# One copy of 64x288 for the partial sums of an output product, four new durations for a planner, and a new instruction order

## The chip, the cores and the metric

The kernel runs on one core of a Trainium2 chip. The metric is device time in microseconds for one launch; several runs are taken and the median is given. The profile is one further execution, recorded by the hardware profiler; its times are in microseconds from the start of its span. TensorE is called PE in the profile (PEld are its weight loads), VectorE DVE, ScalarE ACT, GpSimd POOL, and SP is the engine that issues most of the DMAs.

## The reference, cut to what matters

Two independent computations on the same input `x` (2048 rows of 576 features) are mixed by a gate:

```python
x = A_x
g = sigmoid((x * gate_w).sum(-1, keepdims=True))
a = A(x)      # recurrent, 64 segments
b = B(x)      # ordinary softmax attention
return g * a + (1 - g) * b
```

A is a recurrence. The 2048 rows are cut into 64 segments of 32 rows. Before each segment stand 8 rows of memory, so that 40 rows go in:

```python
for s in range(64):
    h = concat([mem, x[:, 32*s:32*s+32, :]], axis=1)      # 40 x 576
    q, k, v = h @ Wq, h @ Wk, h @ Wv                      # 32 heads of 128
    p = softmax(where(mask, q @ k.T * scale, -1e9))       # 40 x 40 for each head
    o = (p @ v over the heads) @ Wo                       # 40 x 576
    mem = o[:, :8, :]                                     # goes into the next segment
    outs.append(o[:, 8:, :])
```

Only `mem` is passed on: segment s cannot begin with its first 8 rows before the output product of segment s-1 has ended. B is attention over all 2048 rows with 32 heads of 18, and nothing in it depends on A.

## The kernel before, in words

**Two kinds of work in one stream.** A segment of A leaves engines waiting for each other, so the kernel lays B's attention between A's steps. B is 32 chunks (8 groups of 4 heads, times 4 chunks of 512 queries), each of 16 *visits* to 128 keys, 512 visits in all. A visit is `sb` on PE (four matmuls, one for each head, each in its own 32 rows of the array, L932; three write the tile `sb`, one the tile `sp`), then two exponentials on ACT (`ex` 128x1536, L941, and `ey` 128x512, L945), then `ob` on PE (four matmuls in the array's four columns of 32, L955).

**A segment's chain.** Names end in the segment's number, and 0 or 1 in them is the half of the heads.
- `Q0 K0 Q1 K1 V0 V1`, five steps each of four 32-column matmuls of 512 (L1321), into a PSUM bank `pvv`.
- The copy `tm<-pvv` (L540 on DVE, L538 on ACT: both are one helper, `copier`). For Q and K follow a transposing DMA `tt<-tm` (L1411, issued on SP) and a DVE copy `qk<-tt` (L1420); for V one DMA and one copy into `v_sb` (L1360).
- `ph`: scores `psh` (L1435 mask, L1443 products), then an exponential on ACT (L1453). `sm`, `rc`: sums and their reciprocal. `bc`: the reciprocals spread by PE into `prb` (L1487), `nm`: a DVE product (L1498).
- `po`: `pso`, probabilities times values (L1509), `co`: two copies `ot<-pso` of 128x320 (L540 or L538).
- `op`: the output product (L1194). For the first half (`op0`) it is done with two column tiles of 288: four quarters of 32 partitions, of which the two lower hold the sums of the even steps and the two upper those of the odd steps. They have to be added, which is what `halved` does. For the second half (`op1`) it is done with four column tiles of 144, and nothing has to be added.
- `halved` for `op0`: two copies (`su0`, `su1`) bring the upper 64 partitions, 144 columns each, from PSUM to the tile `sum`, and two additions (`tu0`, `tu1`, L1227) add the lower 64 partitions to them. The second half is added by `oc` (`obf<-acc,sum`, L1542).
- `fo`: `pw`, a small fold of the first 8 rows (L1556, L1560) and the DVE product `ht<-pw,keep` (L1568): the memory for the next segment.

The last 8 of the 40 rows do not feed the recurrence. Their output product (`lo`) runs once in four segments and also goes through `halved` (`sl0`, `sl1`, `tl0`, `tl1`, into `lbf`); their projections (`la`, L1025 and L1029) are laid in where there is room.

**What sets the order.** Every operation is first added to a planner, with its engines, a duration in microseconds, its dependencies, a priority, and the buffers it takes and gives back (`tokens_of`: 4 PSUM banks `pb`, 1 `sb`, 2 `sum`, and so on). `Plan.run` then lays the operations out one by one on a clock of its own: at each step it takes the operation that can start first, with priorities among those that start at about the same time. The instructions are emitted in that order, each engine's as one queue. Two numbers are added to the durations: 0.105 when the array's tiling changes (row tiles, column tiles or the whole array, L117), and 0.205 from the end of a PE operation until another engine may use it (L116). Where the plan leaves PE idle it lays in a filler (`warm`, products of a zero tile, L902, planned at 0.216), which keeps PE busy and whose result changes nothing. `TURNS` (L57) has 65 numbers, one for each segment and one ahead: each seeds factors on the priorities and the planner's thresholds until the next segment begins. So any change of one duration can move instructions everywhere behind it.

Two helpers give the planned durations of copies:

```python
def psum_copy(n, narrow=False):
    return ((n / 2 if narrow else n) + 151) / 960.0
def act_time(n):
    return (n + 205) / 1200.0
```

Of the kernel before, what the change touches and what calls it, by code (L numbers as in the profile page):

```python
# [10 lines left out]
FP32 = mybir.dt.float32  # L11
BF16 = mybir.dt.bfloat16
ACT = mybir.ActivationFunctionType
ALU = mybir.AluOpType
# [40 lines left out]
]  # L55
RANK = dict(RANKS[0])
TURNS = [  # L57
    3874553, 4590935, 9148581, 3541498, 535923, 7788852, 3952484, 7153488, 7395194, 8320517, 4368777, 8584864,
    7828412, 8268306, 4467502, 9711640, 4225875, 3218189, 5891388, 9878869, 3366758, 2473878, 665120, 265532,
    2017390, 6740513, 5628863, 269513, 7513788, 1193947, 4221311, 4642080, 2536147, 3044628, 2615070, 8009909,  # L60
    8409899, 7834349, 4105115, 3984977, 6495726, 2668014, 2119719, 693899, 3876392, 7513682, 1436744, 7393048,
    2936900, 4795848, 3391573, 5680957, 6437275, 7165951, 5197151, 4567334, 1419855, 3366056, 6270251,
    7670628, 2126425, 9002684, 6140375, 3882872, 284549,
]
FACTORS = (0.02, 0.1, 0.25, 0.4, 0.55, 0.7, 0.85, 1.0, 1.2, 1.5, 1.9, 2.4, 3.0, 4.0, 6.0, 10.0)
KNOBS = ("switch", "near", "early", "wait", "gap", "cool")
# [44 lines left out]
class Plan:  # L111
# [59 lines left out]
    def add(  # L171
        self, name, engs, dur, fn, deps=(), prio=5.0, mode=None, take=(), give=(), tail=0.0, dmas=0, kb=0.0,
        use=None, pairs=4, alt=None, waits=0.0,
    ):
        op = Op(name, engs, dur, fn, deps, prio, mode, take, give, tail)
        op.dmas, op.kb = dmas, kb
        op.pairs, op.alt, op.form, op.waits = pairs, alt, mode, waits
        op.kind = self.kinds.setdefault(kind_of(name), len(self.kinds))
        op.use = self.ARRAY.get(mode) if use is None else use
        op.seq = len(self.ops)  # L180
        op.slots = {}
        self.ops.append(op)
        return op
# [184 lines left out]
# [6 lines that stand above are left out]
# [3 lines left out]
def kernel(  # L377
# [16 lines left out]
    P = nc.NUM_PARTITIONS  # L394
# [17 lines left out]
    RW = Dm // NF  # L412
# [18 lines left out]
    plan = Plan()  # L431
    add = plan.add
# [29 lines left out]
    for jj in range(2):  # L462
        nc.vector.memset(bsel[64 * jj:64 * jj + 64, jj:jj + 1], 1.0)
    nc.gpsimd.affine_select(
        out=veil[0:64, M:L], in_=veil[0:64, M:L], pattern=[[1, seg]],
# [6 lines left out]
    for j in range(4):  # L472
        r = slice(32 * j, 32 * j + 32)
# [55 lines left out]
    def given(pool, tag, shape, dt):  # L529
        k = plan.slot(tag)  # L530
        return pool.tile(shape, dt, name=tag, tag=f"{tag}{k}", bufs=1)
# [3 lines left out]
    def copier(out_of, in_of):  # L535
        def fn(e):
            if e == "ACT":
                nc.scalar.copy(out=out_of(), in_=in_of())  # L538
            else:
                nc.vector.tensor_copy(out=out_of(), in_=in_of())  # L540
        return fn
# [373 lines left out]
    for gq in range(GB * NQC):  # L915
# [3 lines left out]
        for kb in range(NKB):  # L919
            c = 4 * g + kb // KC  # L920
            o = (kb % KC) * P
            if qc == 0 and kb % KC == 0:
                load_k(c)
                load_v(c)

            def visit(e, c=c, gq=gq, o=o, kb=kb):
                box["sb", gq, kb] = sb = ps_s.tile([P, 3, QC], FP32, name="sb")
                box["sp", gq, kb] = sp = bank([P, QC], FP32, "sp")
                kc, qt_ = kring[c % NKR], qring[gq % NQR]
                for j in range(4):  # L930
                    r = slice(32 * j, 32 * j + 32)
                    nc.tensor.matmul(  # L932
                        sb[:, j, :] if j < 3 else sp[:, :], lhsT=kc[r, o:o + P], rhs=qt_[r, :], start=True, stop=True,
                        tile_position=(32 * j, 0),
                    )

            vi = add(f"sb{gq}.{kb}", "PE", 0.216, visit, [k_of[c], q_of[gq], last_vi], prio=-0.6 if gq < 2 else 0.0, mode="row", take=("sb", "pb"))

            def expo(e, gq=gq, kb=kb):
                box["etb", gq, kb] = etb = given(bint, "etb", [P, 4, QC], BF16)  # L940
                nc.scalar.activation(out=etb[:, 0:3, :], in_=box["sb", gq, kb][:, :, :], func=ACT.Exp, scale=scale_b)  # L941

            def expo4(e, gq=gq, kb=kb):
                etb = box["etb", gq, kb]
                nc.scalar.activation(out=etb[:, 3, :], in_=box["sp", gq, kb][:, :], func=ACT.Exp, scale=scale_b)  # L945

            ex = add(f"ex{gq}.{kb}", "ACT", act_time(1536), expo, [vi], prio=0.0, take=("etb",), give=(("sb", vi, 0),))
            ey = add(f"ey{gq}.{kb}", "ACT", act_time(512), expo4, [ex], prio=0.01, give=(("pb", vi, 0),))

            def values(e, c=c, gq=gq, kb=kb, o=o):  # L950
                if kb == 0:
                    box["ob"] = ps_o.tile([P, QC], FP32, name="ob")
                ob, vc, etb = box["ob"], vring[c % NVR], box["etb", gq, kb]
                for j in range(4):
                    nc.tensor.matmul(  # L955
                        ob[32 * j:32 * j + 32, :], lhsT=vc[:, o + 32 * j:o + 32 * j + 32], rhs=etb[:, j, :],
                        start=(kb == 0), stop=(kb == NKB - 1), tile_position=(0, 32 * j), skip_group_check=True,
                    )
                if kb == NKB - 1:
                    box["ob", gq] = ob  # L960

            va = add(
                f"ob{gq}.{kb}", "PE", 0.216, values, [ex, ey, v_of[c], last_va], prio=-0.5 if gq < 2 else RANK["ob"], mode="col",
                take=("ob",) if kb == 0 else (), give=(("etb", ex, 0),),
            )
            visits[gq, kb] = (vi, ex, va)
            last_vi, last_va = vi, va
            if kb == 0:
                plan.opens.add(va)
            if kb == NKB - 1:  # L970
                plan.closes.add(va)
            if kb == 0:
                first_va = va
            if kb == NKB - 1:
                visits["quse", gq] = vi
            if qc == NQC - 1 and kb % KC == KC - 1:
                visits["kuse", c], visits["vuse", c] = vi, va
# [120 lines left out]
    opened = {}  # L1098
# [73 lines left out]
    plan.tokens_of("tm", 4)  # L1172
    plan.tokens_of("xl", 2)
    plan.tokens_of("obf", 1)
    plan.tokens_of("sum", 2)
    plan.tokens_of("lbf", 1)
    plan.tokens_of("tt", 3)
    plan.tokens_of("xg", 1)
# [30 lines left out]
        return op  # L1209

    def halved(name, state, done, out_of, last_give, prio, held=()):
        lows, sums = [], []

        def low(i):
            def fn(e):
                if i == 0:
                    state["sum"] = given(opened["fix"], "sum", [P, RW], FP32)
                copier(
                    lambda: state["sum"][64 * i:64 * i + 64, :],
                    lambda: state["acc"][64:128, RW * i:RW * i + RW],  # L1220
                )(e)
            return fn

        def both(i):
            def fn(e):
                r = slice(64 * i, 64 * i + 64)
                nc.vector.tensor_tensor(  # L1227
                    out=out_of()[r, :], in0=state["acc"][0:64, RW * i:RW * i + RW], in1=state["sum"][r, :], op=ALU.add,
                )
            return fn  # L1230

        for i in range(2):
            lows.append(add(
                f"s{name[0]}{i}.{name[1:]}", ("DVE", "ACT"), (psum_copy(144), act_time(144)), low(i), [done, *lows], prio=prio,
                take=("sum",) if i == 0 else (),
            ))
        for i in range(2):
            sums.append(add(
                f"t{name[0]}{i}.{name[1:]}", "DVE", 0.308, both(i), [lows[i], *sums], prio=prio, take=held if i == 0 else (),
                give=(("pb", state["op0"], 0), *last_give(lows[0])) if i else (),  # L1240
            ))
        return sums[1], lows[0], sums[0]

    group_end = {}
    pend_lo = []
# [5 lines left out]
    for s in range(n_seg):  # L1251
# [124 lines left out]
        for hf in range(2):  # L1376
# [69 lines left out]
                            start=False, stop=True, tile_position=(0, 32 * i), skip_group_check=True,  # L1446
                        )

            p_ = add(f"ph{hf}.{s}", "PE", 0.365, psh, [*turned, pl], prio=RANK[f"ph{hf}"], mode="col", take=("pb",), use=0.4, pairs=36)
            cur[f"psh{hf}"] = p_  # L1450

            def xp(e, hf=hf, s=s):
# [30 lines left out]
            def bc(e, hf=hf, s=s):  # L1483
                box["prb", s, hf] = pr = bank([P, W8], FP32, "prb")
                for k, o in enumerate(CH):
                    for i in range(4):
# [3 lines left out]
                            rhs=ident[:, :], start=True, stop=True, tile_position=(0, 32 * i), skip_group_check=True,  # L1490
                        )

            b_ = add(f"bc{hf}.{s}", "PE", 0.176, bc, [r_], prio=RANK[f"bc{hf}"],
                     mode="col", take=("pb",), use=0.3, pairs=12)

            def nm(e, hf=hf, s=s):
# [5 lines left out]
            def pso(e, hf=hf, s=s):  # L1502
# [3 lines left out]
                for r in range(8):  # L1506
                    for jj in range(2):
# [4 lines left out]
                            rhs=et[rr, r * L:(r + 1) * L], start=True, stop=True, tile_position=(64 * jj, 0),  # L1512
                        )

            o_ = add(f"po{hf}.{s}", "PE", 0.2, pso, [n_, lv, *pvx], prio=RANK[f"po{hf}"], mode="tall", take=("pb", "pb"), pairs=16, waits=0.15,
                     give=(("tm", evx, 0),))
            cur[f"pso{hf}"] = o_
            for jj in range(2):
# [21 lines left out]

        def ob_cast(e, s=s, st=acc_state, st0=first_half):
            nc.vector.tensor_tensor(  # L1542
                out=opened["obf"][:, s % 4, 0:RW], in0=st["acc"][:, :], in1=st0["sum"][:, :], op=ALU.add
            )

        c1 = add(f"oc{s}", "DVE", 0.308, ob_cast, [mids[1], half_sum], prio=0.3, take=("obf",) if s % 4 == 0 else (),
# [258 lines left out]
```

## Time and profile before

| what | value |
|---|---|
| median of 3 runs | 1424.92 us (1424.34 to 1431.61) |
| profiled execution, its own time | 1423.9 us |
| its span | 1422.0 us, so 1.9 us lie around it |
| PE busy | 1349.8 us, 95% of the span |
| ACT busy | 1097.6 us, 77% |
| DVE busy | 860.2 us, 60% |
| POOL busy | 529.7 us, 37% |
| granted PE clock, mean | 0.996 |
| copies `sum<-acc` 64x144 | 126 on DVE of 310 ns, 34 on ACT of 275 ns |
| additions `sum<-acc,sum` and `lbf<-acc,sum` 64x144 | 160 on DVE of 300 ns |

Busy time of an engine is the union of its instructions. Fillers count as busy, and the ends of matmuls are modelled, so that a PE that is busy 95% is not one that could not do the same work in less. The chain of waits follows the execution back from its last instruction, at each step to what released it.

The span has three stages: projections and preparation up to about 130 us, the 64 segments with B's visits between them from there to about 1395 us, and the final product and the gate's mixing in the last 27 us.

### The profile page before, as it was taken

The page shows a single profiled execution, that of the slowest core. Times are in us where ns is not written, and L with a number is a line of the kernel's source. Part 1 is how long each engine was busy: PE and PEld are TensorE (multiplying, and loading weights), DVE is VectorE, ACT ScalarE, POOL GpSimd, SP SyncE. Part 2 cuts the span into 40 slices and gives each one's busy share as a digit, 9 for nine tenths or more (in the row PEclk, how much of TensorE's full clock was granted, in tenths as well). Part 3 has the DMA queues.
Part 4 walks back from the last instruction along what each step waited for, and adds up shares of the span by engine and source line. Part 5 has one row for each costly group of instructions (what it writes and reads, how often), then busy time and mean ns, then how long its engine had stood idle before and what let it go on. Part 6 is the DMA issues. An engine that isn't in the chain of part 4 may idle for free.

```text
span 1422.0 us, 73418 instructions
## 1 busy us (share of the span) xinstructions
PE 1349.8 (95%) x32607; PEld 717.7 (50%) x32620; DVE 860.2 (60%) x2093; ACT 1097.6 (77%) x1297; POOL 529.7 (37%) x1148
## 2 busy tenths in 40 slices
PE   8999899999999999999999999999999999999998
PEld 4455344555555444555555544555554444444445
DVE  4454466666656656665566666666656666565657
ACT  3478778887887777787877877788777887888884
POOL 8252244234532345332543325333353333432320
PEclk9999999999999999999999999999999999999999
DMA  8887644333424434433433334333335333333335
GB/s 260 249 326 213 134 81 68 63 69 73 78 61 73 57 78 72 71 63 63 83 66 70 64 67 77 73 61 71 63 81 89 59 54 56 66 64 54 54 76 176
DMA packets 343993, 130.66 MB, mean 92 GB/s; under 512 B 296495, under 2 KB 330023, under 8 KB 343675
## 3 DMA queue, kind: packets, MB, share of 16 engines
q1 hardware_dynamic: 315155, 80.47, 29.3%
q0 software_dynamic: 26368, 43.31, 11.2%
q8 instruction: 255, 4.18, 1.3%
q10 hardware_dynamic: 2152, 2.19, 0.5%
q14 instruction: 63, 0.52, 0.1%
HBM read 52.74 MB, written 31.12 MB: 59 GB/s over the span
## 4 chain that ended last, share of the span: by engine, by line
PE 67%; DVE 14%; DMA 11%; issue 3%; ACT 3%; SPq 1%; DVEq 0%; POOL 0%; ACTq 0%; POOLq 0%
PE pvv L1321 25%; PE sb L932 8%; PE acc L1194 8%; DMA tt<-tm 7%; PE ob L955 6%; PE pv L1025 4%; DVE ot L540 3%; PE pso L1509 3%; PE pq L734 2%; DVE tm L540 2%; DMA v_sb<-tm 2%; ACT etb L941 2%; PE pv L1029 2%; DVE sum L540 2%; PE psh L1443 2%
## 5 line engine op out<-in xcount | busy, mean ns | idle before, releaser
L941 ACT ACTIVATE etb<-sb 128x1536 bf16<-128x1536 f32 x512 | 743.6, 1452 | 227.0 <-PE sp L932 156.6
L540 DVE CAST tm<-pvv 128x512 bf16<-128x512 f32 x359 | 247.3, 689 | 238.1 <-PE pvv L1321 233.2
L1321 PEld LDWEIGHTS <-ht 128*32 128x32 bf16 x7680 | 200.8, 96 | 217.2 <-issue 38.5
L945 ACT ACTIVATE etb<-sp 128x512 bf16<-128x512 f32 x512 | 304.1, 594 | 0.6 <-PE sp L932 0.6
L932 PE MATMUL sb<-qch,kch 32*128 32x512 bf16 x1536 | 201.1, 385 | 4.1 <-ACT etb L941 3.4
L955 PE MATMUL ob<-etb,vch 128*32 128x512 bf16 x2048 | 200.5, 384 | 0.5 <-DVE tq L983 0.4
L932 PE MATMUL sp<-qch,kch 32*128 32x512 bf16 x512 | 196.6, 384 | 3.1 <-DMA kch<-ktd 1.7
L1194 PE MATMUL acc<-wo,ot 128*32 128x288 bf16 (+1 forms) x6144 | 169.1, 248 | 6.7 <-DVE ot L540 4.8
L1321 PE MATMUL pvv<-wq_m,ht 128*32 128x512 bf16 x2048 | 145.2, 380 | 2.9 <-DVE ht L1568 0.8
L1321 PE MATMUL pvv<-wv_m,ht 128*32 128x512 bf16 x2048 | 144.0, 380 | 0.3 <-DVE tm L540 0.3
L1321 PE MATMUL pvv<-wk_m,ht 128*32 128x512 bf16 x2048 | 142.8, 380 | 1.4 <-DVE vl L540 0.6
L1194 PEld LDWEIGHTS <-ot 128*32 128x32 bf16 x6144 | 110.8, 96 | 49.5 <-DVE ot L540 26.2
L540 DVE CAST ot<-pso 128x320 bf16<-128x320 f32 x206 | 94.9, 483 | 67.2 <-PE pso L1509 63.4
L932 PEld LDWEIGHTS <-kch 32*128 32x128 bf16 x2048 | 54.5, 91 | 144.6 <-issue 129.2
L1270 POOL COPY ht<-xg 128x96 bf16<-128x96 bf16 x64 | 18.9, 296 | 278.2 <-PE pvv L1321 273.6
L1420 DVE COPY qk<-tt 128x512 bf16<-128x512 bf16 x256 | 77.3, 304 | 40.1 <-DMA tt<-tm 36.6
L851 POOL DMA_DIRECT2D qch<-qtd x120 | 61.9, 523 | 96.2 <-PE sp L932 91.5
L851 POOL DMA_DIRECT2D otd<-stage x124 | 63.2, 517 | 56.2 <-DVE stage L998 39.6
L1498 DVE TENSOR_TENSOR et<-et,prb 128x320 bf16<-128x320 bf16 x128 | 62.0, 485 | 36.5 <-PE prb L1487 29.7
L1453 ACT ACTIVATE et<-psh 128x320 bf16<-128x320 f32 x128 | 56.3, 441 | 32.9 <-PE psh L1443 30.4
L955 PEld LDWEIGHTS <-vch 128*32 128x32 bf16 x2048 | 53.7, 94 | 50.2 <-issue 40.2
L1360 DVE COPY v_sb<-tm 32x512 bf16<-32x512 bf16 x226 | 70.8, 313 | 8.4 <-ACT tm L538 3.2
(161 smaller groups left out, 1972.3 us busy)
## 6 DMA issues: line engine op xcount, KB each, us to landing
v_sb<-tm SPq DMA_DIRECT2D x256, 32.0 KB
xl<-qkd SPq DMA_DIRECT2D x64, 128.0 KB
qkd<-vl POOLq DMA_DIRECT2D x48, 128.0 KB
wo<-in_A_Wo_dram POOLq DMA_DIRECT2D x4, 1152.0 KB
vgd<-vt SPq DMA_DIRECT2D x32, 128.0 KB
wv_m<-in_A_Wv_dram POOLq DMA_DIRECT2D x4, 1024.0 KB
wq_m<-in_A_Wq_dram POOLq DMA_DIRECT2D x4, 1024.0 KB
wk_m<-in_A_Wk_dram POOLq DMA_DIRECT2D x4, 1024.0 KB
```

Source lines behind the costliest of these rows:

```text
L540: nc.vector.tensor_copy(out=out_of(), in_=in_of())
L851: dma(out=rows_, in_=pads) if out else dma(out=pads, in_=rows_)
L932: nc.tensor.matmul(sb[:, j, :] if j < 3 else sp[:, :], lhsT=kc[r, o:o + P], rhs=qt_[r, :], start=True, stop=True, tile_position=(32 * j, 0),)
L941: nc.scalar.activation(out=etb[:, 0:3, :], in_=box["sb", gq, kb][:, :, :], func=ACT.Exp, scale=scale_b)
L945: nc.scalar.activation(out=etb[:, 3, :], in_=box["sp", gq, kb][:, :], func=ACT.Exp, scale=scale_b)
L955: nc.tensor.matmul(ob[32 * j:32 * j + 32, :], lhsT=vc[:, o + 32 * j:o + 32 * j + 32], rhs=etb[:, j, :], start=(kb == 0), stop=(kb == NKB - ...
L1025: nc.tensor.matmul(out_, lhsT=lw, rhs=rw, start=(c == 0), stop=(c == NF), skip_group_check=wide)
L1194: nc.tensor.matmul(acc[32 * q:32 * q + 32, :], lhsT=o[:, slot, t0:t0 + CT], rhs=wo[:, h, d:d + n], start=(first and s_ == (s_ % 2 if wide ...
L1321: nc.tensor.matmul(pv[32 * j:32 * j + 32, :], lhsT=ht[:, cc, :], rhs=rw, start=(c == 0), stop=(c == NF), tile_position=(0, 32 * j), skip_g ...
L1360: move(out=opened["v_sb"][64 * (j // 2):64 * (j // 2) + CT, o:o + 512], in_=tm[32 * j:32 * j + CT, :],)
L1420: eng.tensor_copy(out=opened["qk"][:, hf, a, 0:16 * L].rearrange("p (j i t) -> p j i t", i=4, t=L)[:, :, :, 0:CT], in_=box["tt", s, a, hf] ...
L1498: nc.vector.tensor_tensor(out=et[:, :], in0=et[:, :], in1=box["prb", s, hf][:, :], op=ALU.mult)
```

## The change

Three things are changed. In `halved`, one copy of 64x288 takes the place of the two of 64x144; the tile `sum` is 288 wide instead of 144, there is one of it instead of two, and both additions wait for the one copy. The planner's durations of `sb`, `ph`, `bc` and `po` are set to other values. And `TURNS` has 65 new numbers. The lines that follow in the file have moved up by 9.

```diff
 TURNS = [
-    3874553, 4590935, 9148581, 3541498, 535923, 7788852, 3952484, 7153488, 7395194, 8320517, 4368777, 8584864,
...
+    7952103, 9687964, 5516313, 4619848, 2331426, 9781478, 6767540, 9438387, 4494518, 2665133, 7827388,
...
-            vi = add(f"sb{gq}.{kb}", "PE", 0.216, visit, [k_of[c], q_of[gq], last_vi], prio=-0.6 if gq < 2 else 0.0, mode="row", take=("sb", "pb"))
+            vi = add(f"sb{gq}.{kb}", "PE", 0.3, visit, [k_of[c], q_of[gq], last_vi], prio=-0.6 if gq < 2 else 0.0, mode="row", take=("sb", "pb"))
...
-    plan.tokens_of("sum", 2)
+    plan.tokens_of("sum", 1)
...
     def halved(name, state, done, out_of, last_give, prio, held=()):
-        lows, sums = [], []
-
-        def low(i):
-            def fn(e):
-                if i == 0:
-                    state["sum"] = given(opened["fix"], "sum", [P, RW], FP32)
-                copier(
-                    lambda: state["sum"][64 * i:64 * i + 64, :],
-                    lambda: state["acc"][64:128, RW * i:RW * i + RW],
-                )(e)
-            return fn
+        def low(e):
+            state["sum"] = given(opened["fix"], "sum", [P, 2 * RW], FP32)
+            copier(lambda: state["sum"][0:64, :], lambda: state["acc"][64:128, :])(e)
 
         def both(i):
             def fn(e):
-                r = slice(64 * i, 64 * i + 64)
+                cols = slice(RW * i, RW * i + RW)
                 nc.vector.tensor_tensor(
-                    out=out_of()[r, :], in0=state["acc"][0:64, RW * i:RW * i + RW], in1=state["sum"][r, :], op=ALU.add,
+                    out=out_of()[64 * i:64 * i + 64, 0:RW], in0=state["acc"][0:64, cols], in1=state["sum"][0:64, cols], op=ALU.add,
                 )
             return fn
 
-        for i in range(2):
-            lows.append(add(
-                f"s{name[0]}{i}.{name[1:]}", ("DVE", "ACT"), (psum_copy(144), act_time(144)), low(i), [done, *lows], prio=prio,
-                take=("sum",) if i == 0 else (),
-            ))
+        first = add(
+            f"s{name[0]}0.{name[1:]}", ("DVE", "ACT"), (psum_copy(288) + 0.05, act_time(288)), low, [done], prio=prio, take=("sum",),
+        )
+        sums = []
         for i in range(2):
             sums.append(add(
-                f"t{name[0]}{i}.{name[1:]}", "DVE", 0.308, both(i), [lows[i], *sums], prio=prio, take=held if i == 0 else (),
-                give=(("pb", state["op0"], 0), *last_give(lows[0])) if i else (),
+                f"t{name[0]}{i}.{name[1:]}", "DVE", 0.34, both(i), [first, *sums], prio=prio, take=held if i == 0 else (),
+                give=(("pb", state["op0"], 0), *last_give(first)) if i else (),
             ))
-        return sums[1], lows[0], sums[0]
+        return sums[1], first, sums[0]
...
-            p_ = add(f"ph{hf}.{s}", "PE", 0.365, psh, [*turned, pl], prio=RANK[f"ph{hf}"], mode="col", take=("pb",), use=0.4, pairs=36)
+            p_ = add(f"ph{hf}.{s}", "PE", 0.41, psh, [*turned, pl], prio=RANK[f"ph{hf}"], mode="col", take=("pb",), use=0.4, pairs=36)
...
-            b_ = add(f"bc{hf}.{s}", "PE", 0.176, bc, [r_], prio=RANK[f"bc{hf}"],
+            b_ = add(f"bc{hf}.{s}", "PE", 0.24, bc, [r_], prio=RANK[f"bc{hf}"],
...
-            o_ = add(f"po{hf}.{s}", "PE", 0.2, pso, [n_, lv, *pvx], prio=RANK[f"po{hf}"], mode="tall", take=("pb", "pb"), pairs=16, waits=0.15,
+            o_ = add(f"po{hf}.{s}", "PE", 0.14, pso, [n_, lv, *pvx], prio=RANK[f"po{hf}"], mode="tall", take=("pb", "pb"), pairs=16, waits=0.15,
...
-                out=opened["obf"][:, s % 4, 0:RW], in0=st["acc"][:, :], in1=st0["sum"][:, :], op=ALU.add
+                out=opened["obf"][:, s % 4, 0:RW], in0=st["acc"][:, :], in1=st0["sum"][:, 0:RW], op=ALU.add
```

The copy reads the upper 64 partitions over all 288 columns and writes the tile's lower 64 partitions; the second addition reads columns 144 to 287 of both operands and writes partitions 64 to 127, columns 0 to 143.

## The prediction

> **What bounds the kernel now.** I read the page's busy shares first, then the chain of waits, then the segment stage piece by piece. One per cent of this kernel is 14 us; about 0.5% (7 us) is what a measurement of it can tell from no change.
>
> ```profile
> PE 1349.8 (95%) x32607; PEld 717.7 (50%) x32620; DVE 860.2 (60%) x2093; ACT 1097.6 (77%) x1297; POOL 529.7 (37%) x1148
> PE 67%; DVE 14%; DMA 11%; issue 3%; ACT 3%; SPq 1%; DVEq 0%; POOL 0%; ACTq 0%; POOLq 0%
> PE pvv L1321 25%; PE sb L932 8%; PE acc L1194 8%; DMA tt<-tm 7%; PE ob L955 6%; PE pv L1025 4%; DVE ot L540 3%; PE pso L1509 3%; PE pq L734 2%; DVE tm L540 2%; DMA v_sb<-tm 2%; ACT etb L941 2%; PE pv L1029 2%; DVE sum L540 2%; PE psh L1443 2%
> ```
>
> PE looks full, but the chain is on PE for 67% only: DVE, DMA and ACT hold the other third. The recurrence is a loop in which PE's queue, in its fixed order, meets waits. How much, the chain in order of time shows (start, length, what):
>
> ```profile
> 607.10 1.29 PE pvv L1321 x24
> 608.39 0.32 PE sb L932 x3
> 608.72 0.00 PE sp L932
> 608.72 0.33 PE pvv L1321 x4
> 609.05 0.21 PE ob L955 x4
> 609.26 1.29 PE pvv L1321 x24
> ```
>
> Six groups of four column products take 1.29 us, so one occupies PE 0.215 us; a visit's scores 0.32, which is 0.215 and a change of tiling of 0.105; the group behind them pays 0.105 again. In the same way I read, for operations that wait for nothing, 0.36 for `ph`, 0.177 for `bc`, 0.196 and a change for `po`, 0.25 for a step of `op`, 0.28 for a `la` unit of five. I laid these over the order of PE operations between `fo0` and `fo62` (170.1 to 1372.2 us): 1089 us of work, fillers included, in 1202 us. So 113 us, 1.8 us for each segment of 19.4, PE waits with nothing even to fill. That, and not PE's work, is what an order can change.
>
> The changed copies are in the tail that closes the loop. In DVE's timeline:
>
> ```profile
> 698.15 0.89 DVE L540 CAST ot<-pso 128x320 bf16<-128x320 f32 x2 [0.76 <-PE pso L1509]
> 699.07 0.65 DVE L540 COPY sum<-acc 64x144 f32<-64x144 f32 x2
> 699.75 0.63 DVE L1227 TENSOR_TENSOR sum<-acc,sum 64x144 f32<-64x144 f32 x2
> 700.49 0.31 DVE L1542 TENSOR_TENSOR obf<-acc,sum 128x144 bf16<-128x144 f32 x1
> ```
>
> PE's timeline has the products of the second half over by 699.96; `obf` starts at 700.49 because DVE is at the partial sums until 700.38. `fo` and the next segment's projections wait for `obf`. The reader sees here that DVE, at 60%, is the bound for a stretch of each segment.
>
> **The change part by part.**
>
> *One copy for two.* A copy of 64x144 takes 310 ns on DVE. A PSUM copy of 128x288 (`vt<-pvb`) takes 458 ns, and partitions do not count, so 64x288 takes 0.46. [...] In some segments the copy isn't the last thing before `obf`, and `op1` comes in as the next wait; I take −7. The two additions stay at 0.30 each; the new 0.34 and the 0.05 on the copy exist in the plan only.
>
> On ACT there were 34 such copies of 275 ns; built from its source, the changed program has 11. ACT rows of 275 (144) and 430 (320) put 288 at 0.40, so 9.4 us become 4.4. ACT mostly waits for scores and not the reverse, so this lies beside: −1 (0 to −5). DVE gets 69 copies where it had 126: 39.1 to 31.7 us.
>
> *One `sum` tile for two.* The copy for `lo` may not start while `op0`'s sums are held from the copy to `obf`, 1.4 us or more, and `lo` holds one of four PSUM banks meanwhile; what else waits in DVE's queue then is its next work. This happens in 16 groups at most, so 0 to 16 x 1.4 = 22 us. The plan knows of the tile and lays `lo` elsewhere, so I take a low +1.
>
> *Four durations.* "Set to the trace" is half true. Scores at 606.16 let the exponential start at 606.65, 0.49 later. The plan had 0.216 and its 0.205 for handing over, 0.42; now it has 0.505. `psh` at 612.34 lets its exponential start at 612.97, 0.63 against 0.57 before and 0.615 now. So the hand-over to other engines is now right. But a duration is also how long PE is held, and there the old numbers were right (0.216, 0.365, 0.176, 0.2 against my 0.22, 0.36, 0.177, 0.196) and three new ones are long: 512 x 0.084 + 128 x 0.045 + 128 x 0.064 − 128 x 0.06 = 49 us that PE won't need, 0.8 for each segment. The real PE reaches its next operation earlier than planned, and then waits.
>
> *The order.* From the programs: fillers (four products of the zero tile each) 174 to 138, changes of tiling 1330 to 1292, 37 `la` parts from one full form to four column forms (20 weight loads where there were 5, +0.003 each by the rows, nothing). Between `fo0` and `fo62` the same rows give 1081.8 us of PE work where there were 1089.3: −7.5. On POOL there are 14 more `v_sb` copies at 0.62, on DVE 14 fewer at 0.31; SP's DMA into the same tile takes 3 to 5 us beside them, which hides them as long as the other half comes by DMA. SP's and POOL's DMAs are as many as before (893 instructions on SP in both).
>
> Against the shorter stream stands what lies between a step and the next one that needs it. For each hand-off I took the time, from start to start on PE, that about a tenth of the cases in the trace of before undercut, and summed by how much the PE work that the order lays between is less: from the last K product to `ph` 5.20 us (half 0: short by 0.2 us in sum before, 1.8 after; half 1: 4.1 and 9.6), from V to `po` 4.9 (12.6 and 17.5), from scores to `ob` 2.64 (31.4 and 42.8), scores to scores 2.12 (29.0 and 28.1), through `sm`, `bc`, `po`, `op` and `fo` 40.7 and 43.1. All in all 118 us before, where 113 were really waited: the count is sound in size. After: 143. The growth is what the long durations make: a visit between two steps covers 0.084 less than planned. But a wait at one place covers the others, above all where many small ones meet, so of the growth of 24.9 I count the 11.4 of scores to `ob` half: 13.5 + 5.7, times 113/118, +18.5 (0 to +24).
>
> *Fewer fillers and the clock.* The windows show what PE was granted:
>
> ```profile
> 570.00:790.00 220.00, 211.43 (x5580) 117.71 (x5576) 135.39 (x328) 175.79 (x212) 83.46 (x178) 1.00 0.38 70
> 790.00:1010.00 220.00, 210.88 (x5555) 114.72 (x5542) 141.72 (x346) 172.11 (x205) 79.88 (x171) 1.00 0.36 69
> ```
>
> The column after the brackets is the clock, 1.00. The longest waits of PE in this stage by the view of waits:
>
> ```profile
> PE psh L1443 <- DVE qk L1420: 9.2, 19, 1.3
> PE prb L1487 <- DVE rq L1479: 7.3, 16, 1.0
> ```
>
> 1.3 us at most. [...]
>
> **The sum.** −7 − 1 + 1 − 7.5 + 18.5 = +4, and +1 for the POOL copies where they are last. The profiled execution took 1423.9, span 1422.0 and 1.9 around it; its own time becomes 1428.9. The median shown is 1.0 above it: 1429.9, so 1430. The first 130 and last 27 us keep their DMA and product bounds; I give them 0.
>
> **The rivals.**
>
> *Faster: the waits don't grow.* If the right hand-over times let the search place the recurrence's steps well, the shortfalls I counted fall beside waits that are there anyway. For it: exponentials waited for scores 289 times, 156.6 us, and those times are now planned right. Against: covers at `ph` are shorter in the order as it stands. Then −7 − 1 − 7.5 = −15.5, median 1409. It decides below 8 us of growth.
>
> *Slower: the hand-offs add in full.* PE reaches `ph1`, `po` and `ob` early, queues up behind transposes and exponentials, `sb` behind it comes late to ACT, and `op1` ends after the partial sums, so that the copy's saving is gone too. Place: between K's last product and `ph`, where the page has `DMA tt<-tm` at 7% already. +24 − 7.5 + 1 + 1 = +18.5, median 1443. It decides from 15 us of growth. [...]
>
> *The copy alone counts:* the plan's errors cancel over 64 segments, −8: 1417.
>
> **How the numbers follow.** The forecast 0.45 (1421 to 1439: 0.06 faster, 0.20 same, 0.19 slower), the waits don't grow 0.25 (0.23 faster, 0.02 same), in full 0.22 (slower), copy alone 0.08 (half faster, half same). Together 0.33, 0.26, 0.41. Both signs hold much, so the range goes from below 1409 to above 1443, by the sizes of the unknown tile and the rounding of the 2%: 1406 to 1450. 1430 is the likeliest case, not a mean.
>
> **What would show it.** Right: a copy of 64x288 at 0.46 on DVE, `DVE sum L540` in the chain down by a quarter; `fo`'s wait for `obf` (29.7 us, 58 times) shorter; `psh` and `pso` waiting longer; fillers 138; clock 1.00. Wrong: `DMA tt<-tm` not above 7% and a PE that waits under 113 us between `fo0` and `fo62` (the faster rival), or over 135 (the slower one); `lo`'s copy waiting for `obf` would show the single tile; a clock below 0.98 in any window the fillers.

## The result, and the profile after

Over 20 runs each, the kernel after takes 1422.45 us in the median (1415.71 to 1426.65), the kernel before 1427.28 (1420.84 to 1431.61). The ratio is 0.9967, 95% interval 0.9951 to 0.9983: some 5 us faster, a real gain, but a third of a per cent, where a loss of 5 us against the median then shown was forecast. The profiled execution of after took 1421.8 us (span 1420.0).

The shares of busy time and the chain by engine, from the page of after:

```profile
PE 1345.2 (95%) x33172; PEld 720.4 (51%) x33184; DVE 848.2 (60%) x2019; ACT 1091.4 (77%) x1277; POOL 535.4 (38%) x1162
PE 17%; DVE 4%; DMA 4%; ACT 1%; issue 1%; SPq 0%; DVEq 0%; ACTq 0%
```

PE's busy time is the same share as before. The shares of the chain add to 28% only: it could be followed back through a good quarter of the span, so no line of it can be set beside the chain of before. The copies can, by the view of one tile (first row DVE, second ACT: count, then shortest, median and longest ns):

```profile
L540 DVE COPY sum<-acc x69: 458/459/461, 171.3 to 1393.1; 64x288 f32<-64x288 f32 x69
L538 ACT COPY sum<-acc x11: 395/396/400, 190.7 to 869.6; 64x288 f32<-64x288 f32 x11
```

69 copies at 0.459 on DVE and 11 at 0.396 on ACT: count and length are what was forecast. The tail of the segment that the prediction showed, in DVE's timeline of after:

```profile
696.93 0.89 DVE L540 CAST ot<-pso 128x320 bf16<-128x320 f32 x2 [0.60 <-PE pso L1500]
697.85 0.46 DVE L540 COPY sum<-acc 64x288 f32<-64x288 f32 x1
698.34 0.61 DVE L1219 TENSOR_TENSOR sum<-acc,sum 64x144 f32<-64x144 f32 x2
699.06 0.31 DVE L1533 TENSOR_TENSOR obf<-acc,sum 128x144 bf16<-128x144 f32 x1
```

From the end of the `ot` casts to the start of `obf` it is 1.24 us where it was 1.45: 0.21 less. Who feels it, the waits of PE in the stage from `fo0` to `fo62` say (us in total, times, longest). First before, then after:

```profile
PE pw L1556 <- DVE obf L1542: 7.1, 21, 1.0
```

```profile
PE psh L1434 <- DVE qk L1411: 10.0, 22, 1.0
PE prb L1478 <- DVE rq L1470: 8.3, 20, 1.0
PE pw L1547 <- DVE obf L1533: 2.8, 8, 0.7
```

`fo` (tile `pw`) waits 4.3 us less for `obf`; `ph` and `bc` (tiles `psh` and `prb`) wait about 1 us more each than the 9.2 and 7.3 before. Laid over PE's order in the prediction's way (us; the work is the sum of the prediction's times for each step, and the waits are what is left of the stage):

| | start to `fo0` | `fo0` to `fo62` | PE work in it | waits in it | rest |
|---|---|---|---|---|---|
| before | 170.1 | 1202.0 | 1089.2 | 112.8 | 49.8 |
| after | 172.9 | 1195.3 | 1081.8 | 113.6 | 51.8 |

The stage gained 6.7 us, all of it PE work; the waits stayed; ahead of the stage and behind it 4.8 us were given back. One profile is a thin base for such sums: three executions below with the same order in the stage spread over 9 us in it. So the experiments are read by their ratios, and the stage only where ratios point the same way.

### The profile page after: what moved, and what is told of

The parts are those of the page before. It is cut to its first block, busy times and chain, and to the rows that moved or that the text cites. A ratio compares the mean times of both kernels' runs of the same rounds, so it can differ in the third digit from the quotient of the medians.

```text
span 1420.0 us, 74484 instructions
## 1 busy us (share of the span) xinstructions
PE 1345.2 (95%) x33172; PEld 720.4 (51%) x33184; DVE 848.2 (60%) x2019; ACT 1091.4 (77%) x1277; POOL 535.4 (38%) x1162
## 3 DMA queue, kind: packets, MB, share of 16 engines
q0 software_dynamic: 26368, 43.31, 11.4%
## 5 line engine op out<-in xcount | busy, mean ns | idle before, releaser
L1194 PE MATMUL acc<-wo,ot 128*32 128x288 bf16 (+1 forms) x6144 | 165.7, 248 | 7.3 <-issue 3.6
L1312 PE MATMUL pvv<-wq_m,ht 128*32 128x512 bf16 x2048 | 142.1, 380 | 3.9 <-DVE ht L1559 1.5
L540 DVE CAST ot<-pso 128x320 bf16<-128x320 f32 x200 | 91.6, 484 | 58.3 <-PE pso L1500 57.3
L540 DVE CAST vl<-pv 128x512 bf16<-128x512 f32 x84 | 57.2, 685 | 38.8 <-PE pv L1025 21.8
```

The costliest lines, as they stand in the source:

```text
L1194: nc.tensor.matmul(acc[32 * q:32 * q + 32, :], lhsT=o[:, slot, t0:t0 + CT], rhs=wo[:, h, d:d + n], start=(first and s_ == (s_ % 2 if wide ...
L1312: nc.tensor.matmul(pv[32 * j:32 * j + 32, :], lhsT=ht[:, cc, :], rhs=rw, start=(c == 0), stop=(c == NF), tile_position=(0, 32 * j), skip_g ...
```

## The experiments

All kernels but two have their order pinned. The planner's result is written out as a list of operations, each with its engine, its tiling and its buffers, and the program is emitted from the list, so that one part can be changed and all else stands:

```diff
-        for op in self.run():
+        for name, eng, form, slots in LAID:
+            op = byname[name].pop(0)       # "warm": a new filler in this form
+            op.eng, op.form, op.slots = eng, form, slots
...
```

Ratios are to the kernel before, run beside each on the same chip.

### The copy without the order, the order without the copy

one_copy: the order of before; the second copies leave the list, the first become 64x288 into one tile (the change's own hunks of `halved`, `sum` and `ob_cast`).

```diff
-["su0.s", ..., {"sum": [0 or 1]}] ["su1.s", ...]
+["su0.s", ..., {"sum": [0]}]
```

> The order of before is written out and kept (same engines, same places, same 181 fillers); only the two copies of 64x144 become one of 64x288, in one tile, at the place of the first. Theory of the prediction: the tail before obf shortens by 0.19 us in most segments, -7 us, so a ratio of about 0.995. Rival (the copy is hidden and the new order is what gained): within 2 us of before, 0.9985 to 1.0015. If the copy alone gives more than the whole change (-4.7 us), the new order costs something.

Measured: 1415.11 us, ratio 0.9928 (0.9906 to 0.9950).

two_copies: the order of after; each 64x288 copy is two of 64x144 again, in the old two tiles, everything else as in after.

```diff
-["su0.s", ..., {"sum": [0]}]
+["su0.s", ..., {"sum": [0]}] ["su1.s", ...]
```

> The order of the changed kernel is written out and kept; the one copy of 64x288 is two copies of 64x144 again, the second right behind the first on the same engine. Theory of the prediction: the order by itself costs +11 us (waits +18.5, PE work -7.5), ratio 1.008. Rival A (copy and order give about half each): -0 to -2 us, 0.9985 to 1.000. Rival B (the copy is hidden): -4.7 us as the whole change, 0.997.

Measured: 1428.81 us, ratio 1.0010 (0.9994 to 1.0026). So the copy alone gives more than the whole change, and the new order alone gives nothing that can be told from zero. PE's waits for `obf` in the stage, in one_copy and then in two_copies:

```profile
PE pw L1558 <- DVE obf L1544: 1.4, 6, 0.4
```

```profile
PE pw L1567 <- DVE obf L1553: 7.3, 21, 0.7
```

So `fo` waits 7.1 us for `obf` in before and 7.3 in two_copies, and 1.4 in one_copy and 2.8 in after. (One_copy's first fold, which waits 0.8, lies just ahead of the window and would make it 2.2.) Not all of that is the merging: the control below, two copies into one wide tile, has 4.6 in 14 waits. From 1.0010 to 0.9967 the copy is worth 0.43% in the new order, 0.72% in the old one; with intervals of 0.2% on each, these do not clearly differ.

### Which copies bring it

The order of before again, and only some of its pairs merged. In merge_dve these are the 59 pairs with both copies on DVE, in merge_act the 21 with at least one on ACT (13 merged copies stand on ACT, 8 on DVE). two_new_layout is the control: no pair merged, but the wide tile and its placement.

```diff
+MERGED = [...]        # 59 names, 21 names, none
+        whole = name in MERGED
...
+                c = slice(0, 2 * RW) if whole else slice(RW * i, RW * i + RW)
+                copier(lambda: state["sum"][0:64, c], lambda: state["acc"][64:128, c])(e)
```

> The order of before written out; only the 59 pairs of copies that both ran on DVE are one copy of 64x288 each, the 21 pairs with one or both on ACT stay two copies of 64x144. In the single copy of all pairs (one_copy, 0.9928) the segment stage went from 1202.0 to 1191.4 us. Theory: 59 x 0.19 us on DVE's tail gives -7 of these, ratio 0.995. Rival: the pairs with ACT carry most, because a copy on ACT waits for DVE with the exponentials behind it: here only -3 us, 0.998.

> The complement: the order of before, only the 21 pairs with a copy on ACT are merged (onto the engine of the first), the 59 pairs on DVE stay two copies. Theory of the tail on DVE: 8 pairs lose a hop from DVE to ACT and back and 13 lose one ACT copy of 0.275 for 0.12 more, -2 to -3 us, 0.998. Rival, the exponentials behind ACT's copies: -6 to -7 us, 0.995.

> A control for merge_dve and merge_act: the order of before, no pair merged, but the one tile of 64x288 and its new placement (both copies into the lower 64 partitions, the second addition writes across). Theory that only merging matters: 0.9985 to 1.0015. Rival, that the placement itself frees waits between DVE and ACT: -3 us or more, below 0.998.

Measured: merge_dve 0.9952 (0.9931 to 0.9973), merge_act 0.9952 (0.9932 to 0.9971), two_new_layout 0.9983 (0.9965 to 1.0001). In us, the control −2.4 (not clear of zero), and beyond it −4.4 each for the 59 pairs and for the 21. They add with the control to −11.2, and one_copy measured −10.3. By the middle values a pair with a member on ACT is worth nearly three times as much as one on DVE, −4.4/21 = −0.21 us against −4.4/59 = −0.07; each −4.4 has about 4 us on either side, so that this ratio is not settled. What may lie behind it, a segment of before shows in the timeline of all engines:

```profile
621.04 0.31 DVE L540 COPY sum<-acc 64x144 f32<-64x144 f32 x1
621.39 0.30 DVE L1227 TENSOR_TENSOR sum<-acc,sum 64x144 f32<-64x144 f32 x1
621.77 0.28 ACT L538 COPY sum<-acc 64x144 f32<-64x144 f32 x1 [0.54 <-DVE sum L1227]
622.07 1.45 ACT L941 ACTIVATE etb<-sb 128x1536 bf16<-128x1536 f32 x1
622.08 0.30 DVE L1227 TENSOR_TENSOR sum<-acc,sum 64x144 f32<-64x144 f32 x1 [0.40 <-ACT sum L538]
...
623.58 0.39 PE L932 MATMUL sb<-qch,kch 32*128 32x512 bf16 x3 [0.40 <-ACT etb L941]
```

DVE copies and adds the first half; ACT stands idle for 0.54 us until it may copy the second, with an exponential of 1.45 us queued behind; DVE then stands 0.40 us for ACT, and PE's next scores 0.40 us for the exponential. One copy removes this crossing. Over the whole program the view of the tile `sum` counts how long an engine sat idle until an ACT copy had ended, and the view of waits how long the scores `sb` waited for an exponential in the stage (us, times, longest). Before, then merge_act:

```profile
  ACT sum L538: 5.4, 15
PE sb L932 <- ACT etb L941: 3.4, 9, 0.8
```

```profile
  ACT sum L550: 1.5, 4
PE sb L944 <- ACT etb L953: 1.0, 4, 0.3
```

The control stands where before does in both, at 5.2 us in 14 waits and 3.4 in 9, so these two are the merged pairs' own. `fo` is not: it waits 4.7 us for `obf` in merge_act, but 4.6 in the control too. And a single copy on ACT is not what costs: 13 of merge_act's merged copies still stand there, and head_tail_dve below moves 12 of them to DVE and gains nothing. What is left is the second hop between the engines; no run takes out that alone.

### Does PE's work count, and do shorter covers?

Sixty fillers of four products (0.216 us each, 13.0 us in all), one to a segment, are put into one_copy's order, at three places in three kernels: right ahead of `ph1`, in the middle of the second half's Q product, and (58 of them, 12.5 us) right behind `sm1`.

```diff
+["warm", "PE", "col", {}]
 ["ph1.10", "PE", "col", {"pb": [1]}]
```

> One copy in the order of before (one_copy), with 60 more fillers of 0.216 us, one in each segment, right ahead of ph1, where PE waits for transposes (K to ph1 short by 25 us in sum). The prediction counted a lack of cover as lost time: this adds cover just there, so it is free, 0.993 as one_copy. If PE's work counts wherever it stands: +13 us, 1.002.

> The same 60 fillers in the middle of Q1, where PE waits for nothing. If PE's work there is on the path: +13 us on one_copy, 1.002. If waits later in the segment swallow it (a wait is a sum over what came before, and not a sum of places): +0 to +5 us, 0.993 to 0.9965.

> One copy in the order of before, with 58 more fillers of 0.216 us right behind sm1, where PE waits for the reciprocal and for the probabilities (sm1 to bc1, bc1 to po1) and where the plan puts most of its own. If work is on the path ahead of ph1 only: +0 to +4 us on one_copy, 0.993 to 0.996. If PE's work counts everywhere: +13 us or more, 1.002 to 1.004, as fill_ph1 and fill_mid.

Measured: 1.0041 (1.0024 to 1.0057), 1.0029 (1.0011 to 1.0046) and 1.0002 (0.9991 to 1.0013). Against one_copy's 0.9928 this is +16, +14 and +10.6 us. Work added ahead of `ph1`, the step that waits 20 times in one_copy's view and where I thought it free, cost its full length and no less than in the middle of a product; only behind `sm1` may a little of it be hidden. So the 7.4 us that the new order takes off PE's work should be worth about 7 us.

early_ph1: the reverse. In 36 segments one PE step that stood right ahead of `ph1` goes right behind it, so that about 9 us less work covers the way from K to `ph1`; nothing is added.

```diff
-["ob8.1", "PE", "col", {}]
 ["nm0.11", "DVE", null, {}]
 ["ph1.11", "PE", "col", {"pb": [3]}]
+["ob8.1", "PE", "col", {}]
```

> One copy in the order of before (one_copy, 0.9928); in 36 segments the PE step that stood right ahead of ph1 (16 steps of la, 12 of lo, 7 ob, 1 V1; 0.216 to 0.285 us) stands right behind it, about 9 us less cover between K1 and ph1 in sum, total work kept. Theory of the prediction: PE waits for the transposes instead, +3 to +6 us, 0.995 to 0.997. Rival, that all PE work ahead of ph1 is on the path of the recurrence and that behind it is not: up to -9 us, 0.987 to 0.990. Third: the transposes bind in most of these, 0.993 as one_copy.

Measured: 0.9972 (0.9954 to 0.9989), 0.44% or 6 us above one_copy, with 0.28% on either side. The waits of PE, early_ph1's over the whole program, have `ph` at the top. First one_copy, then early_ph1:

```profile
PE psh L1445 <- DVE qk L1422: 8.9, 20, 1.6
```

```profile
PE psh L1445 <- DVE qk L1422: 11.1, 22, 1.8
```

The `psh` row rises by 2 us only; where the other 4 us go, one profile does not show. A shorter cover at this place does cost, by the middle values some two thirds of what it is short by.

### The fillers

before_nofill and after_nofill: each kernel's own order without its fillers (174 and 138 groups of four column products; 155 and 126 of them stand in the stage, where PE's work falls by 33 and 27 us).

```diff
-["warm", "PE", "col", {}]        # all 174, or all 138
```

> The order of before with its 174 column fillers left out, nothing else moved. If PE's work counts in full, 174 x 0.216 = -37.6 us (0.974). If the fillers stand only where PE has to wait anyway, within 2 us (0.9985 to 1.0015). If they keep the clock up, more half-clock windows than the three inside before's span after 50 us, each costing up to 1.7 us: slower.

> The order of the changed kernel with its 138 column fillers left out. PE's work in full: -29.8 us on the changed kernel (0.976 of before); fillers free: as the changed kernel, 0.9967; clock lost: slower than the changed kernel, with more half-clock windows in the profile.

Measured: 1.0063 (1.0042 to 1.0083) for before; 0.9993 (0.9973 to 1.0014) for after, 0.26% above after itself, at the edge of what can be told. To take 33 us of empty work off before's PE makes the kernel 9 us slower. Part of the reason is in the windows (busy us of PE and of the other engines, then the granted clock, DMA share, GB/s), before_nofill:

```profile
570.00:790.00 220.00, 206.82 (x5476) 116.47 (x5468) 132.09 (x319) 172.48 (x210) 82.03 (x175) 0.98 0.35 68
...
1010.00:1230.00 220.00, 199.53 (x5178) 104.21 (x5176) 133.32 (x333) 169.03 (x199) 79.76 (x171) 0.97 0.37 65
```

Both of before's windows in the prediction, the first of them over the same stretch, were at 1.00. Over all runs the mean granted clock was 0.995 in before, 0.9845 in before_nofill, 0.993 in after and 0.991 in after_nofill; with a clock of 1.00 or 0.50 at any time, as in the traces of before and after, PE stands at half clock for 13 to 15 us of an execution of before, 44 of before_nofill, 20 of after, 26 of after_nofill (an estimate from these means). In before_nofill's profile 27 us of half clock fall in the stage, which cost up to 14 us, half of them. The stage takes 1210.4 us there, 8.4 more than in before; so of the 33 us that were taken out some 28 come back as longer waits (an estimate from this one profile), and the clock makes the rest of the loss. In before the fillers held the clock, 1.00 with them and 0.98 without from 570 to 790 us; but between before and after, 174 or 138 makes no difference in the stage that can be told (after's profile has one stretch of 3.4 us at half clock in it, as one_copy's with 174 has). A window of after:

```profile
570.00:790.00 220.00, 213.94 (x5744) 118.86 (x5736) 138.12 (x325) 176.64 (x209) 83.39 (x179) 1.00 0.36 71
```

### Head, stage and tail of the order

head_before is two_copies' order with one copy, but with before's order up to `fo0`; head_tail_before has before's order behind `fo62` as well; head_tail_dve is the same with the 12 `su`/`sl` copies that stood on ACT on DVE.

```diff
-LAID = order of after
+LAID = order of before up to fo0, then that of after [, from fo62 that of before]
...
-["su0.0", "ACT", null, {"sum": [0]}]
+["su0.0", "DVE", null, {"sum": [0]}]
```

> One copy everywhere. Up to the end of the first segment's fold the order of before, from there the order of the changed kernel. The changed kernel's profile lost 2.8 us ahead of that fold, where a copy on DVE waits 8.5 us for a transposing DMA and PE behind it 5.8 us, and half-clock time follows. Theory that the new order loses in the first stage: -3 us on the changed kernel, about 0.995 of before. Rival (the loss is one execution's, or is made up by later waits): as the changed kernel, 0.9967.

> The order of before up to the first fold and after the last one (fo62), the order of the changed kernel between, one copy everywhere. The changed order lost 2.8 us at the head and 2 to 4 at the end in its profiles. Theory: both losses go, -3 to -4 us on head_before, 0.990 to 0.991. If the end's loss is no property of the order: as head_before, 0.993.

> head_tail_before (0.9921) with its remaining copies of sums on ACT put on DVE in their places. The 21 pairs with ACT gave as much as the 59 on DVE; if a copy on ACT costs because exponentials stand behind it, another -2 us, 0.991. If DVE's tail grows as much by them: as head_tail_before, 0.992.

Measured: 0.9931 (0.9904 to 0.9958), 0.9921 (0.9902 to 0.9940) and 0.9919 (0.9898 to 0.9941). With before's head, the new order in the stage does as well as the old one in one_copy (0.9928), and no better. After itself has 0.9967, against 0.9924 as the mean of these three: its head costs some 5 us (0.43% of 1427 is 6, with about 3 on either side; head_before alone says 5). The tail and the last copies on ACT cost nothing that can be seen. The stage of these three, with the same order but for 12 engines, took 1185.2, 1194.4 and 1186.6 us in their profiles: this is the 9 us of swing. What is late in the head, DVE's and then PE's timeline of after show:

```profile
148.10 0.29 DVE L1411 COPY qk<-tt 128x512 bf16<-128x512 bf16 x1 [8.46 <-DMA tt<-tm]
148.68 1.29 DVE L540 CAST vl<-pv 128x512 bf16<-128x512 f32 x2 [0.28 <-DMA vld<-vl]
```

```profile
149.42 0.58 PE L932 MATMUL sp<-qch,kch 32*128 32x512 bf16 x1 [5.75 <-DVE vl L540]
149.93 0.62 PE L955 MATMUL ob<-etb,vch 128*32 128x512 bf16 x4
```

PE stands 5.75 us for a `vl` copy, which frees PSUM, and comes back at half clock (0.51 granted from 147.60 to 151.00; 0.58 and 0.62 us for matmuls that took 0.38 and 0.40 at 141 us). The copy stands behind a `qk` copy whose DMA transpose is under way for 8.46 us. But that is not what holds it: the second row says that `vl` then waits for a DMA of its own, `vld<-vl`, which has to empty its buffer and lands at 148.55. Without the `qk` copy ahead it would hardly have started sooner. Late is the DMA. SP issues these transfers from 141.40 on in after, behind a transpose, and from 139.31 on in before:

```profile
141.40 2.16 SPq L1083 DMA_DIRECT2D vld<-vl  x3
```

```profile
139.31 2.25 SPq L1083 DMA_DIRECT2D vld<-vl  x3
142.56 0.69 DVE L540 CAST vl<-pv 128x512 bf16<-128x512 f32 x1 [1.52 <-DMA vld<-vl]
```

In before the first of them has landed by 142.44, and one `vl` copy gets through at 142.56; the next waits there too, 4.51 us, until 147.75. In after the first lands 7.2 us after its issue, beside loads that keep the DMA share at 1.04 and 1.08 from 140.8 to 147.6; why it takes so long is not shown further. The stall belongs to the order: in two_copies and after_nofill, with the same head, PE stands 4.98 and 4.59 us here, and 0.8 to 3.6 in the twelve with before's head and fillers (2.40 in head_before). How all of the 5 us come about stays open. `fo0` starts at 172.9 us in the profiles of after and two_copies, and at 168.2 to 174.1, 171.0 in the mean, in those twelve: that is 2 us.

### Durations and seeds

old_durations: after, with the four old durations and its own `TURNS`; old_turns: after with its new durations and before's `TURNS`. Both are planned anew.

```diff
-            vi = add(f"sb{gq}.{kb}", "PE", 0.3, visit, ...
+            vi = add(f"sb{gq}.{kb}", "PE", 0.216, visit, ...
...
-TURNS = [7952103, ...]
+TURNS = [3874553, ...]
```

(the first hunk, and 0.365, 0.176, 0.2 in the same way, for old_durations; the second for old_turns)

> The changed kernel with the four durations of before (0.216, 0.365, 0.176, 0.2) and its own TURNS. The plan lays 334 column fillers where the changed one has 138. No theory of mine gives its size: the seeds were not searched for these durations. If a searched order matters most, several per cent slower than before; if the durations in themselves make better hand-overs, slower than the old_turns kernel (new durations with seeds that were not searched for them either), which is to follow.

> The changed kernel with the 65 TURNS of before: one copy and the new durations, with seeds that were not searched for them (266 column fillers). Beside old_durations (1.0565), which has the changed kernel's seeds and the old durations. If the search of the seeds carries the order: 3 to 7% slower than before. If the new durations carry it: under 1% from the changed kernel.

Measured: 1.0565 (1.0540 to 1.0590) and 1.0462 (1.0433 to 1.0490), with 334 and 266 fillers where after has 138. In the profile of old_durations PE is busy for 1402.4 us, 57 more than in after, and still idle for 7% of the span. The new durations do not make a good order by themselves, nor do the seeds: seeds that were found for one set of durations did not carry over to the other, in either direction. What the new durations bring with a search of their own, against the old ones with a search of theirs, cannot be split further by these runs, beyond that the order as a whole comes to 1.0010. A search with the old durations and the one copy was not tried.

## Why the prediction was wrong, step by step

- *What bounds the kernel.* Right as far as tested: PE's work and its waits between `fo0` and `fo62` add to the time, and work counts at full length (the fillers, +16, +14, +10.6 us).
- *The copy on DVE, −7.* About right. The copy of 64x288 takes 0.459 us, as the 0.458 of 128x288 in before said. With its gap it is 0.49 (697.85 to 698.34 in after) where a pair was 0.68 (699.07 to 699.75 in before), and this is the 0.19 that the expectations use. The −7 itself was my estimate and no run shows it alone: `fo`'s wait is down by some 4 to 5 us, a part of it in the control too; merge_dve measured −6.8 (0.48%), beyond the control −4.4.
- *The copy on ACT, −1.* Too small: −4.4. The step "ACT mostly waits for scores, so this lies beside" took the mean of a stage for the place of the copy. In the segment shown an exponential is queued behind the copy, and the copy itself waits for DVE. The low end that I gave, −5, holds it.
- *One `sum` tile, +1.* Not seen: the control with the single wide tile measured −2.4, not clear of zero.
- *PE work, −7.5.* The same count over after's trace gives −7.4. That such work is worth its length is what the fillers showed.
- *The waits, +18.5.* This is the step that failed: they grew by some 4 to 8 us. two_copies, with the new order and the old copies, has 120.8 us of waits in its stage where before had 112.8: +8.0 by one profile. With one copy, the four profiles of the new stage (after and the three of the head) have 108.6 in the mean and one_copy 102.2: +6. By two_copies' ratio (+1.4 us), with −7.5 of work and +5 for the head, it is 4. The fault is in the "needed" times. I took for scores to `ob` the 2.64 us that a tenth of the cases in before undercut. That number is not how long scores, exponential and hand-over take; it is how close the old order usually put the two. The new order puts them at 2.49 us in a tenth of its cases. The page of before already spoke against it: I counted PE short by 31.4 us there, and the row has PE idle for 0.5 us ahead of all 2048 matmuls of `ob` (after: 0.3; the row stands below this list), where only waits of under 0.17 us could hide, behind the end of a group that is shown for 0.385 us and occupies PE for 0.215. That my sum, 118, came near the 113 waited was luck in this term. With the lower of the two traces for each hand-off, the same sum grows by 14.2 and not by 24.9: scores to `ob` −1.0 (I had +11.4), K to `ph1` +4.5, V to `po` +7.6. That a shorter cover costs, early_ph1 shows: 9 us less ahead of `ph1` cost 6. The mechanism was right, and its size two to four times too large.
- *What was to be seen.* `fo` waits less, `psh` longer, `pso` longer for `et` (2.5 to 4.0 us) and shorter for `v_sb` (2.7 to 1.6). PE's waits in the stage at 113.6 lie at the border of the faster rival's sign (under 113) and far from the forecast's 131. `DMA tt<-tm` can't be judged, since after's chain is cut short.
- *Head and tail, 0.* Wrong for the head: some 5 us, by head_before and the two beside it; I had kept the first 130 us at their bounds, and the stall lies between there and `fo0`, in a stretch that stood in none of my terms.
- *Fillers and clock, no term in the sum.* Right in the stage for 174 against 138: 1.00 from 570 to 790 us in both. That no wait of before was over 1.3 us there, which the prediction shows beside it, was not a reason: the last section has a drop of the clock with no gap over 0.73.

PE at `ob`, from the page of before (busy us, mean ns of one, then idle us ahead of it):

```profile
L955 PE MATMUL ob<-etb,vch 128*32 128x512 bf16 x2048 | 200.5, 384 | 0.5 <-DVE tq L983 0.4
```

With the measured terms: −4.4 − 4.4 − 2.4 − 7.5 + 8 = −10.7, and +5 for the head, −5.7 on 1427.28. Measured: −4.8. The agreement is looser than it looks: the same terms without the copy give two_copies +5.5, and it measured +1.4 (−0.9 to +3.7). Of the rivals, "the copy alone counts" (1417) came nearest, and it was given 0.08: the order by itself is worth nothing that can be told from zero, and the copy about 6 us in it. "The waits don't grow" had the sign, but the waits did grow, towards its border of 8 us.

The best kernels here are one_copy, head_before, head_tail_before and head_tail_dve, 0.9919 to 0.9931 and alike within their intervals. All four beat both before and after: the copy in one, and either order for the stage, but before's head.

## What to carry to other kernels

A time read as "the least that lies between two steps" from a trace is a latency only if the schedule ever tried to go below it; take it from a chain in which each step starts as soon as the one ahead of it ends, or from two schedules, and see whether the engine is idle at that place at all. A small operation on an engine with idle time need not be free if it waits for another engine and a long one is queued behind it (in before 0.28 us on ACT ahead of 1.45): look at the queue at that place, not at the engine's share. Where a copy waits behind another copy, see what it waits for once that has gone. When an order is searched anew, compare head, stage and tail by themselves: a gain in 64 segments can be half lost in one stall ahead of them.

## What the runs showed of the hardware

Windows of 3.4 us ahead of a drop of the clock and behind it, in before (the number after the last bracket is the granted clock):

```profile
159.08:162.50 3.42, 1.49 (x60) 0.76 (x62) 0.59 (x2) 1.89 (x3) 1.27 (x3) 1.00 0.38 104
162.50:165.90 3.40, 3.40 (x74) 1.44 (x68) 1.54 (x4) 2.40 (x3) 2.02 (x4) 0.50 0.52 65
```

PE is busy for 1.49 of 3.42 us, its longest gap there is 1.96 us, and the next 3.40 us run at 0.50. In before_nofill a drop stands in the stage, behind one wait of `ph` (windows, then PE's timeline):

```profile
687.60:691.40 3.80, 2.12 (x81) 1.36 (x79) 0.66 (x4) 1.74 (x5) 1.93 (x4) 1.00 0.30 94
691.40:694.80 3.40, 3.01 (x68) 1.50 (x68) 1.75 (x5) 3.23 (x5) 1.26 (x3) 0.50 0.44 46
```

```profile
690.16 0.38 PE L1454 MATMUL psh<-qk 128*32 128x40 bf16 x32 [1.68 <-DVE qk L1431]
```

PE is busy for 2.12 of 3.80 us (1.73 in the last 3.41 of them), with a gap of 1.68. The drop at 947.39 in the same trace has 2.32 us busy in the 3.41 ahead of it, and no gap over 0.73. So the granted clock went to 0.50 behind stretches whose longest gaps were 1.96, 1.68 and 0.73 us.

How busy PE was in the window tells more in these traces than its longest gap. In each of the 18 the drops lie on a grid of 3.41 us; those of before at 46.45, 53.28 and 162.51 us last 3.41 us each, at 0.50. Of all windows of that grid at full clock, from 60 to 1395 us, 24 had PE busy for under 1.5 us, and all 24 were followed by half clock; of 123 with 1.5 to 2.4 us 25 were; of 6818 with more, one (in before and after alone 4 of 4, none of 8, none of 764). What decides in the middle band is not shown. So before_nofill paid for its missing fillers at gaps not far from those of before: 1.68 and 0.73 us were the longest ahead of these two drops, and 1.3 is the longest wait in the prediction's view.
